# Longer load packets, an earlier start, later weight transfers and a shifted attention schedule in a fused window-attention and softplus-layer kernel

## The chip, the cores and the metric

The kernel runs on one core of a Trainium2 chip. The metric is device time in microseconds (us) of one execution.

The engines are named as the profile names them: PE is TensorE's matmuls, PEld its weight loads, DVE is VectorE, ACT is ScalarE, POOL is GpSimd and SP is SyncE, which mostly issues transfers (SPq is its issuing queue). "Granted clock" (PEclk) is the share of full speed that TensorE was given.

## The reference

Eight batches of attention with 8 heads, 576 positions and head size 64. A position sees a window of 32 to each side; eight "global" positions see everything and are seen by all. The result, as 4608 tokens of 512 features, goes through two matrix products with a softplus between them.

```python
scores = scale * np.matmul(q, k.transpose(0, 1, 3, 2))
mask = np.abs(pos[:, None] - pos[None, :]) <= 32
mask = mask | is_global[:, None] | is_global[None, :]
scores = np.where(mask, scores, -1000000000.0)
... # softmax over keys
x = np.matmul(attn, v)          # -> 4608 tokens x 512
h = x @ w_in                    # 512 -> 2048
g = np.maximum(h, 0.0) + np.log1p(np.exp(-np.abs(h)))
return g @ w_out                # 2048 -> 512
```

## The kernel before

The 4608 tokens are handled as nine tiles of 512 (tile 0 to tile 8). A tile has 16 slots. In slot `s` of tile `n` the kernel emits one sixteenth of the first layer of tile `n` (`mm1`: four 512-column matmuls and two ScalarE passes), one sixteenth of the second layer of tile `n - 1` (`mm2`), and some attention steps of a later batch. Batch 0 must be done before tile 0, batch 1 before tile 1, and so on. Four parts matter here.

All of k, q and v are loaded by position, one head after another, so each contiguous piece is 64 fp32 numbers, 256 bytes:

```python
def load(n, b, eng=None):
    for t in range(NTL):
        s0 = KW * t
        eng.dma_start(out=stage[n][:ST[t], t].rearrange("p (h d) -> p h d", d=D),
                      in_=src[n][b, :, s0:s0 + ST[t], :].rearrange("h s d -> s h d"))
```

There is one staging buffer for each of k, q and v; GpSimd casts it to bf16, and only then can the next batch be loaded into it:

```python
for i, n in enumerate("kqv"):
    at((-22, -20, -17)[i], 1, load, n, b)
    at((-22, -20, -17)[i], 1, load_rows, n, b)
    for t in range(NTL):
        at(-12 + i + t // 3, 0, cast_tile, n, b, t, nc.gpsimd)
for p in range(NP):                      # four pairs of heads
    s = 4 * p - 8
    at(s, 1, transposes, "k", b, p)
    at(s + 1, 0, transposes, "q", b, p)
    at(s + 2, 1, scores, b, p, 0)        # ... exp, mask
    at(s + 4, 1, sums, b, p)             # matmuls with ones
    at(s + 4, 1, values, b, p)           # matmuls with V: these need the cast of v
    ...
    at(s + 5, 1, scale_x, b, p)          # writes xT
at(11, 0, glob_out, b)                   # last writes of xT: tile b waits for them
```

The weights: `w_in` is issued by GpSimd before batch 0's attention, `w_out` just after it, ahead of tile 0:

```python
glob_out(0)
...
for c in range(4):
    nc.gpsimd.dma_start(out=w_out_t[:, 4 * c:4 * c + 4, :], in_=moe_w_out[...])
```

The main loop. In tile 0 there is no second layer, and batch 1 runs at double pace:

```python
for n in range(n_tiles + 1):
    for s in range(16):
        if n < n_tiles: mm1(n, s)
        if n == 0:
            for r in (2 * s - 12, 2 * s - 11):
                attend(1, r, 0); attend(1, r, 1)
            ...                              # and the first steps of batches 2 and 3
            continue
        for b in (n + 1, n + 2, n + 3): attend(b, s - 16 * (b - n - 1), 0)
        mm2(n - 1, s)
        for b in (n + 1, n + 2, n + 3): attend(b, s - 16 * (b - n - 1), 1)
```

The softmax here doesn't subtract the row's maximum and nothing guards it: scores larger than these inputs give would overflow.

Of the kernel before, what the change touches and what calls it, by code (L numbers as in the profile page):

```python
# [11 lines left out]
FP32 = mybir.dt.float32  # L12
# [7 lines left out]
P = 128  # L20
WIN = 32
KW = 120
# [7 lines left out]
SPLIT = 288  # L30

# [6 lines left out]
def kernel(  # L38
# [12 lines left out]
    NP = H // 2  # L51
    d_model, d_ff = moe_w_in.shape
# [16 lines left out]
    ones = const.tile([P, D], BF16)  # L69
    xT = const.tile([P, KD, B * S], BF16)  # L70
# [4 lines left out]
    V1 = [const.tile([P, NTL, d_model], BF16, name=f"V1_{i}") for i in range(2)]  # L75
    stage = {n: const.tile([P, NTL, d_model], FP32, name=f"{n}_f") for n in "kqv"}
    ident_bf = const.tile([P, P], BF16)
    src = {"k": k, "q": q, "v": v}
    grow = {n: nc.dram_tensor(f"{n}_global_rows", (NG, B * H * D), FP32, kind="Internal").ap() for n in "kqv"}


    def load(n, b, eng=None):
        eng = eng or nc.sync
        for t in range(NTL):
            s0 = KW * t
            eng.dma_start(out=stage[n][:ST[t], t].rearrange("p (h d) -> p h d", d=D),  # L86
                          in_=src[n][b, :, s0:s0 + ST[t], :].rearrange("h s d -> s h d"))

    def load_rows(n, b, eng=None):
        eng = eng or nc.sync  # L90
        g = grow[n][:, b * H * D:(b + 1) * H * D]
        eng.dma_start(out=stage[n][KW:P, 0:4], in_=g.unsqueeze(1).to_broadcast([NG, 4, H * D]))
        eng.dma_start(out=stage[n][ST[4]:ST[4] + NG, 4], in_=g)

    def gather(n, eng, regs):
        sv = src[n].rearrange("b h s d -> (b h) s d")
        for g in range(NG):
            eng.dma_start(out=grow[n][g:g + 1].rearrange("o (c d) -> c o d", d=D),
                          in_=sv[:, bass.ds(regs[g], 1), :])
# [3 lines left out]
    def cast_tile(n, b, t, eng):  # L103
        if n == "v":
            kqb[n, b] = V1[b % 2]
        elif t == 0 and b:
            kqb[n, b] = work.tile([P, NTL, d_model], BF16, tag=f"{n}b", bufs=2, name=f"{n}b")
        rows = ST[t] if b == 0 and n != "v" else P
        eng.tensor_copy(kqb[n, b][:rows, t], stage[n][:rows, t])  # L109


    gidx = global_idx.rearrange("(one n) -> one n", one=1).bitcast(I32)
    nc.sync.dma_start(out=idx_r[:], in_=gidx)
    nc.scalar.dma_start(out=idx_i[:], in_=gidx.to_broadcast([P, 2 * NG]))
    nc.scalar.preload_act_table_set("natural_log_exp_and_others")
    for n in "kqv":
        nc.gpsimd.memset(stage[n][96:P, 4], 0.0)
    load("k", 0)
    load("q", 0)

    for n in "kq":
        kqb[n, 0] = work.tile([P, NTL, d_model], BF16, tag=f"{n}b", bufs=2, name=f"{n}b")
        nc.vector.memset(kqb[n, 0][96:P], 0.0)

    ident = work.tile([P, P], FP32, tag="ot", bufs=2, name="ident")
    make_identity(nc, ident[:])
    nc.vector.tensor_copy(ident_bf[:], ident[:])
    nc.vector.memset(ones[:], 1.0)
    low = work.tile([P, NG, NG], FP32, tag="m0")
    nc.gpsimd.memset(low[:], 1.0)  # L130
    nc.gpsimd.affine_select(out=low[:], in_=low[:], compare_op=ALU.is_ge, fill=0.0, base=-1,
                            channel_multiplier=0, pattern=[[1, NG], [-1, NG]])
    kidx_i = work.tile([P, NTL], I32, tag="m3")
    nc.gpsimd.iota(kidx_i[:], pattern=[[KW, NTL]], base=0, channel_multiplier=1)
    vld = const.tile([P, NTL], FP32)
    nc.gpsimd.memset(vld[:], 1.0)
    dgs = []
    for i, (s, c) in enumerate(((KW, slice(0, 4)), (ST[4], slice(4, 5)))):
        nc.gpsimd.affine_select(out=vld[:, c], in_=vld[:, c], compare_op=ALU.is_ge, fill=0.0, base=s - 1,
                                channel_multiplier=-1, pattern=[[0, c.stop - c.start]])  # L140
        dg = work.tile([P, NG], FP32, tag=f"m6{i}")
        nc.gpsimd.memset(dg[:], 1.0)
        nc.gpsimd.affine_select(out=dg[:], in_=dg[:], compare_op=ALU.is_equal, fill=0.0, base=-s,
                                channel_multiplier=1, pattern=[[-1, NG]])
        dgs.append(dg)

    band = work.tile([P, 200], FP32, tag="m7")
    nc.gpsimd.memset(band[:], 1.0)
    nc.gpsimd.memset(band[:, 32:40], 0.0)
# [10 lines left out]
    regs = [  # L160
        nc.values_load(idx_r[0:1, 2 * g:2 * g + 1],
                       engines=[mybir.EngineType.Activation, mybir.EngineType.Pool],
                       min_val=0, max_val=S - 1,
                       skip_runtime_bounds_check_because="positions of the sequence")
        for g in range(NG)
    ]
    gather("v", nc.scalar, regs)
    gather("k", nc.gpsimd, regs)
    gather("q", nc.gpsimd, regs)
    load("v", 0)  # L170
    load_rows("v", 0, nc.scalar)

# [3 lines left out]

# [3 lines left out]
    nc.vector.tensor_tensor(out=same[:], in0=same[:], in1=low[:], op=ALU.mult)  # L180
    uq = work.tile([P, NG], FP32, tag="m2")
    nc.vector.tensor_reduce(out=uq[:], in_=same[:], axis=AX.X, op=ALU.max)
    nc.vector.tensor_scalar(out=uq[:], in0=uq[:], scalar1=-1.0, scalar2=1.0, op0=ALU.mult, op1=ALU.add)

    kidx = work.tile([P, NTL], FP32, tag="m4")
    nc.vector.tensor_copy(kidx[:], kidx_i[:])
    keq = work.tile([P, NTL, NG], FP32, tag="m5")
    nc.vector.tensor_tensor(out=keq[:], in0=kidx[:].unsqueeze(2).to_broadcast([P, NTL, NG]),
                            in1=idx_f[:].unsqueeze(1).to_broadcast([P, NTL, NG]), op=ALU.is_equal)
    onehot = const.tile([P, NTL, NG], BF16)  # L190
    nc.vector.tensor_copy(onehot[:], keq[:])
    akey = const.tile([P, NTL], FP32)
    nc.vector.tensor_reduce(out=akey[:], in_=keq[:], axis=AX.X, op=ALU.max)
    nc.vector.tensor_scalar(out=akey[:], in0=akey[:], scalar1=-1.0, scalar2=1.0, op0=ALU.mult, op1=ALU.add)
    ukey = const.tile([P, 2], FP32)
    for i, dg in enumerate(dgs):
        nc.vector.tensor_tensor(out=dg[:], in0=dg[:], in1=uq[:], op=ALU.mult)
        nc.vector.tensor_reduce(out=ukey[:, i:i + 1], in_=dg[:], axis=AX.X, op=ALU.max)
    nc.vector.tensor_tensor(out=akey[:], in0=akey[:], in1=vld[:], op=ALU.mult)
    masks = [const.tile([P, GW[i]], BF16, name=f"mask{i}") for i in range(2)]  # L200
    for t in range(NTL):
        m = masks[0 if t in GRP[0] else 1]
        c0 = GOFF[t] - (WLO[t] - (128 * t - 40))
        a, vl, u = akey[:, t:t + 1], vld[:, t:t + 1], ukey[:, t // 4:t // 4 + 1]
        if t > 0:
            nc.vector.tensor_scalar(out=m[:, c0:c0 + 40], in0=band[:, 0:40], scalar1=a, scalar2=None, op0=ALU.mult)
        n = ST[t]
        nc.vector.tensor_scalar(out=m[:, c0 + 40:c0 + 40 + n], in0=band[:, 40:40 + n], scalar1=a, scalar2=u,
                                op0=ALU.mult, op1=ALU.add)
        nc.vector.tensor_scalar(out=m[:, c0 + 40 + n:c0 + 48 + n], in0=band[:, 160:168], scalar1=vl, scalar2=None,  # L210
                                op0=ALU.mult)
        if t < 4:
            nc.vector.tensor_scalar(out=m[:, c0 + 168:c0 + 200], in0=band[:, 168:200], scalar1=a, scalar2=None,
                                    op0=ALU.mult)



    def transposes(n, b, p, copy=nc.vector.tensor_copy):
        dst, rows = KT if n == "k" else QT, kqb[n, b]
        ps = psum["pool"].tile([P, 512], FP32, tag="tp", bufs=2 if b == 0 else 1, name="tp")  # L220
        tb = ps[:].bitcast(BF16)
        for t in range(NTL):
            nc.tensor.transpose(out=tb[:, t * P:(t + 1) * P], in_=rows[:, t, p * P:(p + 1) * P], identity=ident_bf[:])  # L223
        if b == 0:
            g = ps[:, 384:384 + NG]
            for t in range(NTL):
                nc.tensor.matmul(out=g, lhsT=rows[:, t, p * P:(p + 1) * P], rhs=onehot[:, t, :],
                                 start=(t == 0), stop=(t == NTL - 1), skip_group_check=True)
        copy(dst[:, p].rearrange("p t c -> p (t c)"), tb[:, 0:NTL * P])  # L229
        if b == 0:  # L230
            copy(dst[:, p, 0:4, KW:P], g.unsqueeze(1).to_broadcast([P, 4, NG]))
            copy(dst[:, p, 4, ST[4]:ST[4] + NG], g)

    exps = {}

    def region(b, name):
        tag, bufs = ({"sc": ("sc", 1), "av": ("av", 2)}[name]) if b == 0 else ("at", 2)
        return psum["pool"].tile([P, 1024], FP32, tag=tag, bufs=bufs, name=name)
# [18 lines left out]

# [63 lines left out]

    gts = {}
# [28 lines left out]
    def attention_slots(b):  # L351
        sl = {}

        def at(s, half, f, *a):
            sl.setdefault((s, half), []).append((f, a))

        for i, n in enumerate("kqv"):
            at((-22, -20, -17)[i], 1, load, n, b)
            at((-22, -20, -17)[i], 1, load_rows, n, b)
            for t in range(NTL):  # L360
                at(-12 + i + t // 3, 0, cast_tile, n, b, t, nc.gpsimd)
        for p in range(NP):
            s = 4 * p - 8
            at(s, 1, transposes, "k", b, p)
# [127 lines left out]
```

## Time and profile before

| | before |
|---|---|
| time, median of 3 runs (range) | 407.64 us (406.65 to 408.45) |
| span of the profiled run | 405.2 us |
| first first-layer matmul (tile 0 can begin) | 44.1 us |
| first second-layer matmul | 103.0 us |
| TensorE busy | 344.7 us |
| packets of all transfers | 124,388 |

The page of the kernel before shows the span in 40 slices of about 10 us. Each digit is a busy share in tenths; for PEclk, the granted clock.

```profile
PE   0367563857999999999999999999999999999985
PEclk9999665798999999999999999999999999999999
DMA  8999999999408771796378558720000101010021
```

For the first 100 us TensorE is only partly busy and the transfers run nearly without a break. After that TensorE is full to the end. So there are three stages: the start, up to the first matmul of tile 0; tile 0; and the rest, where TensorE binds.

The table of windows, cut at the starts of the tiles, puts numbers to this. A tile's start is taken here as its first softplus pass on ScalarE's timeline. The columns are the stretch, its length, the busy time of PE, PEld, DVE, ACT and POOL with instruction counts, the granted clock, the share of the transfer engines (the times of all packets over the time of 16 engines; packets overlap in the records, so it can pass 1), and GB/s. The rows are tile 0, tiles 1 and 2 together, and all that follows.

```profile
core 0: us, PE busy (x) PEld busy (x) DVE busy (x) ACT busy (x) POOL busy (x), PEclk, DMA share, GB/s
46.00:103.90 57.90, 38.32 (x310) 18.41 (x308) 22.04 (x56) 35.49 (x54) 27.70 (x50) 0.78 1.13 189
103.90:179.50 75.60, 73.25 (x605) 37.09 (x604) 34.81 (x92) 61.75 (x97) 17.57 (x42) 1.00 0.58 112
179.50:405.20 225.70, 214.20 (x1468) 103.37 (x1467) 72.56 (x183) 158.55 (x251) 28.89 (x72) 1.00 0.32 74
```

In tile 0 TensorE idles 57.9 − 38.3 = 19.6 us; in tiles 1 and 2 only 2.35 us. What holds tile 0 shows on GpSimd's timeline (start, length, line, operation, count, and in brackets the idle time before it and what ended it):

```profile
42.05 2.04 POOL L319 COPY xT<-xg 128x4 bf16 x8 [15.68 <-DVE xg L314]
44.19 2.97 POOL L436 DMA_DIRECT2D w_out_t<-in_moe_w_out_dram  x4
...
66.33 2.83 POOL L109 CAST V<-v_f 128x512 bf16<-128x512 f32 x5 [12.48 <-DMA v_f<-v_global_rows]
```

The first line finishes batch 0. The second issues all of `w_out`. The third is the cast of batch 1's v, which waited 12.5 us for a transfer and began at 66.3 us.

Last, the page's group of the second layer's matmuls and its queue line. The second layer waited 9.7 us for VectorE's copy of the previous result out of PSUM (`ot`); the packets of queue 1, 118,778 of them with 39.48 MB, took 50.0% of the 16 transfer engines' time over the span.

```profile
q1 hardware_dynamic: 118778, 39.48, 50.0%
...
L343 PE MATMUL o<-w_out_t,gt 128*128 128x512 bf16 x576 | 145.7, 379 | 9.7 <-DVE ot L347 9.7
```

### The profile page before, as it was taken

To read this page: it belongs to the slowest core of one execution; us is meant where nothing else is said; L and a number is where in the kernel's file an instruction comes from. 1 tells how busy PE (TensorE), PEld (TensorE's weight loads), DVE (VectorE), ACT (ScalarE), POOL (GpSimd) and SP (SyncE) were. 2 spreads that over 40 slices of the span, in tenths; PEclk is the share of its full clock that TensorE was granted. 3 is DMA by queue.
4 is the path that set the end of the run, shared out by engine and by line. 5 is a ranking of instruction groups with operands and counts; after the bars stand their busy time and mean duration, and the time that the engine had idled before them with its cause. 6 is when DMAs were issued, how large, how long until landed. Compare 5 with 4: busy or idle time off the path is not lost.

```text
span 405.2 us, 7015 instructions
## 1 busy us (share of the span) xinstructions
PE 344.7 (85%) x2600; PEld 171.5 (42%) x2600; DVE 156.3 (39%) x423; ACT 273.1 (67%) x429; POOL 98.6 (24%) x223
## 2 busy tenths in 40 slices
PE   0367563857999999999999999999999999999985
PEld 0145221433544455455445444444444444444432
DVE  8457120565444444544444444444444201010111
ACT  1068340877988787787878887888788766776600
POOL 5960722364500431234042204220100100000000
PEclk9999665798999999999999999999999999999999
DMA  8999999999408771796378558720000101010021
GB/s 140 206 196 193 185 198 186 177 199 184 82 26 152 152 166 40 153 168 133 77 147 166 93 105 161 160 56 26 28 27 28 53 26 53 28 44 33 28 78 52
DMA packets 124388, 44.60 MB, mean 110 GB/s; under 512 B 114514, under 2 KB 118866, under 8 KB 124354
## 3 DMA queue, kind: packets, MB, share of 16 engines
q1 hardware_dynamic: 118778, 39.48, 50.0%
q0 software_dynamic: 4736, 4.46, 6.6%
q8 instruction: 20, 0.33, 0.3%
q10 hardware_dynamic: 840, 0.22, 0.3%
q14 instruction: 14, 0.11, 0.1%
HBM read 38.90 MB, written 9.83 MB: 120 GB/s over the span
## 4 chain that ended last, share of the span: by engine, by line
PE 63%; ACT 9%; DVE 9%; issue 8%; DMA 5%; SPq 4%; POOL 1%; ACTq 1%; DVEq 0%; POOLq 0%
PE o L343 28%; PE hp L329 22%; ACT ex L250 7%; PE av L273 6%; DVE ot L347 5%; SPq L86 4%; PE tp L223 4%; PE sc L246 3%; DVE ex L255 3%; DMA q_f<-q_global_rows 2%; DMA q_f<-in_q_dram 1%; DMA v_global_rows<-in_v_dram 1%; DMA v_f<-v_global_rows 1%; ACT QT L383 1%; POOL V L109 1%
## 5 line engine op out<-in xcount | busy, mean ns | idle before, releaser
L329 PE MATMUL hp<-xT,w_in_t 128*128 128x512 bf16 x576 | 154.1, 393 | 3.8 <-POOL xT L319 3.8
L343 PE MATMUL o<-w_out_t,gt 128*128 128x512 bf16 x576 | 145.7, 379 | 9.7 <-DVE ot L347 9.7
L332 ACT ACTIVATE e<-hp 128x512 f32<-128x512 f32 x144 | 86.1, 598 | 63.7 <-PE hp L329 61.3
L333 ACT ACTIVATE gt<-e 128x512 bf16<-128x512 f32 x144 | 90.7, 630 | 4.6
L343 PEld LDWEIGHTS <-gt 128*128 128x128 bf16 x576 | 55.2, 97 | 77.6 <-issue 18.8
L329 PEld LDWEIGHTS <-w_in_t 128*128 128x128 bf16 x576 | 53.5, 100 | 69.1 <-issue 15.1
L255 DVE TENSOR_TENSOR ex<-ex,mask 128x1008 bf16<-128x1008 bf16 x64 | 43.7, 684 | 54.2 <-ACT ex L250 53.2
L250 ACT ACTIVATE ex<-sc 128x1008 bf16<-128x1008 f32 x64 | 56.1, 920 | 4.7 <-PE sc L246 4.6
L347 DVE COPY ot<-o 128x512 f32<-128x512 f32 x36 | 24.7, 686 | 72.5 <-PE o L343 72.5
L319 POOL COPY xT<-xg 128x4 bf16 x64 | 12.9, 202 | 141.2 <-DVE xg L314 137.8
L291 ACT ACTIVATE rz<-av 128x616 f32<-128x616 f32 x32 | 21.8, 683 | 19.2 <-DVE KT L229 14.6
L109 POOL CAST V<-v_f 128x512 bf16<-128x512 f32 x40 | 23.8, 644 | 42.1 <-DMA v_f<-v_global_rows 36.0
L246 PE MATMUL sc<-QT,KT 64*128 64x200 bf16 (+2 forms) x320 | 21.3, 258 | 9.9 <-DVE xT L306 2.8
L304 DVE TENSOR_TENSOR xT<-av,rz 128x480 bf16<-128x480 f32 x32 | 21.0, 656 | 22.0 <-ACT rz L295 21.9
L229 DVE COPY KT<-tp 128x640 bf16<-128x640 bf16 x32 | 15.6, 486 | 32.8 <-PE tp L223 32.8
L109 POOL CAST qb<-q_f 128x512 bf16<-128x512 f32 x35 | 20.9, 642 | 29.9 <-DMA q_f<-q_global_rows 25.5
L223 PE MATMUL tp<-ident_bf,kb 128*128 128x128 bf16 x160 | 16.8, 233 | 12.2 <-DVE kb L109 10.4
L273 PE MATMUL av<-ex,V 128*64 128x200 bf16 (+4 forms) x384 | 19.7, 236 | 8.4 <-POOL V L109 7.8
L273 PE MATMUL av<-ex,ones 128*64 128x200 bf16 (+4 forms) x384 | 20.4, 239 | 4.8 <-DVE ex L255 4.7
L282 DVE TENSOR_REDUCE gs<-av 128x8 f32<-128x32 f32 x64 | 11.9, 185 | 31.8 <-ACT rz L291 31.5
L223 PE MATMUL tp<-ident_bf,qb 128*128 128x128 bf16 x160 | 17.2, 234 | 7.5 <-DVE qb L109 5.0
L295 ACT ACTIVATE rz<-rz 128x616 f32<-128x616 f32 x32 | 22.5, 704 | 0.2
(69 smaller groups left out, 167.4 us busy)
## 6 DMA issues: line engine op xcount, KB each, us to landing
out_dram<-ot SPq DMA_DIRECT2D x36, 256.0 KB
k_f<-in_k_dram SPq DMA_DIRECT2D x32, 240.0 KB
q_f<-in_q_dram SPq DMA_DIRECT2D x32, 240.0 KB
v_f<-in_v_dram SPq DMA_DIRECT2D x32, 240.0 KB
w_in_t<-in_moe_w_in_dram POOLq DMA_DIRECT2D x4, 512.0 KB, 12.2
w_out_t<-in_moe_w_out_dram POOLq DMA_DIRECT2D x4, 512.0 KB, 12.2
k_f<-in_k_dram SPq DMA_DIRECT2D x8, 192.0 KB
q_f<-in_q_dram SPq DMA_DIRECT2D x8, 192.0 KB
```

What stands on the lines that cost most here:

```text
L109: eng.tensor_copy(kqb[n, b][:rows, t], stage[n][:rows, t])
L223: nc.tensor.transpose(out=tb[:, t * P:(t + 1) * P], in_=rows[:, t, p * P:(p + 1) * P], identity=ident_bf[:])
L246: nc.tensor.matmul(out=sc[:, e, GOFF[t]:GOFF[t] + w], lhsT=KT[r, p, t, :], rhs=QT[r, p].rearrange("p t c -> p (t c)")[:, WLO[t]:WHI[t]], s ...
L250: nc.scalar.activation(out=ex[:], in_=sc[:, :, 0:GW[grp]], func=ACTF.Exp, scale=SCALE)
L255: nc.vector.tensor_tensor(out=ex[:], in0=ex[:], in1=masks[grp][:].unsqueeze(1).to_broadcast([P, 2, GW[grp]]), op=ALU.mult)
L273: nc.tensor.matmul(out=av[64 * e:64 * e + 64, OFF + lo:OFF + hi], lhsT=weights(t, e), rhs=exps[p, grp][:, e, c:c + hi - lo], start=(lo in ...
L295: nc.scalar.activation(out=RZ[p][:], in_=RZ[p][:], func=ACTF.Exp, scale=-1.0)
L329: nc.tensor.matmul(out=hp[:], lhsT=w_in_t[:, kd, kf * P:(kf + 1) * P], rhs=xT[:, kd, n * NT:(n + 1) * NT], start=(kd == 0), stop=(kd == KD ...
L332: nc.scalar.activation(out=e[:], in_=hp[:], func=ACTF.Exp)
L333: nc.scalar.activation(out=gts[n][:, kf, :], in_=e[:], func=ACTF.Ln, bias=1.0)
L343: nc.tensor.matmul(out=op[:], lhsT=gts[n][:, kf, i * P:(i + 1) * P], rhs=w_out_t[:, kf, :], start=(kf == 0), stop=(kf == KF - 1))
L347: nc.vector.tensor_copy(ot[:], op[:])
```

## The change

The intent, in five points.

1. k and q are loaded as runs of six tokens, 1536 contiguous bytes, instead of 256. v stays as it was. Since a partition now holds six positions, the transposes become six of 96 columns, and the copies out of PSUM are strided; the global columns of later batches come from one table that is built in slot 12 of tile 0.
2. Batch 0 is loaded, cast and computed one pair of heads at a time, so that its scores can begin after the first pair.
3. `w_in` is issued inside batch 0's attention, and `w_out` in slots 1 and 3 of tile 0.
4. From batch 4 on each attention step is one slot later, so that VectorE's mask does not stand ahead of the output copy. Batches 2 and 3 are squeezed to double pace.
5. Ten junk matmuls run before batch 0's first transposes and ten before tile 0, to warm the clock.

The core of the diff, with cuts marked:

```diff
+    def load_runs(n, b, heads=slice(0, H)):
+        nc.sync.dma_start(out=runs[n][:, heads], in_=src[n][b, heads].rearrange("h (p r) d -> p h (r d)", r=RUN))
...
-        for t in range(NTL):
-            nc.tensor.transpose(out=tb[:, t * P:(t + 1) * P], in_=rows[:, t, p * P:(p + 1) * P], identity=ident_bf[:])
+        for r in range(RUN):
+            nc.tensor.transpose(out=tb[:, r * NQ:(r + 1) * NQ], in_=rows[:, r, p * P:(p + 1) * P],
+                                identity=ident_bf[:NQ, :NQ])
...
+    LOAD = {2: (2, 3, 5), 3: (20, 20, 20), 4: (30, 30, 31)}
+    CAST = {1: 1, 2: 16, 3: 26}
+    START = {1: 6, 2: 20, 3: 30}
...
-            s = 4 * p - 8
+            r = 4 * p - 7
...
+                if b in START:
+                    at(START[b] + (r + 7) // 2, (r + 7) % 2, f, *a)
+                else:
+                    at(g0 + r, half, f, *a)
...
+    warm(10)
     transposes("k", 0, 0)
...  # batch 0, pair by pair; load_w_in(p) inside; batch 1's k and q issued at p == 1
     glob_out(0)
+    load_v(1)
+    load_v_rows(1)
+    for n in "kq":
+        gather(n, nc.sync)
+    load_global_columns()
+    warm(10)
...
-    for c in range(4):
-        nc.gpsimd.dma_start(out=w_out_t[...], in_=moe_w_out[...])
...
     for n in range(n_tiles + 1):
         for s in range(16):
             if n < n_tiles:
                 mm1(n, s)
+            if n == 0 and s in (1, 3):
+                load_w_out(s - 1)
+                load_w_out(s)
+            if n == 0 and s == 12:
+                for m in "kq":
+                    global_columns(m)
+            attend(16 * n + s, 0)
+            if n:
+                mm2(n - 1, s)
+            attend(16 * n + s, 1)
```

## The prediction

> **What bounds the kernel now.** Three stages, read from the timeline. (1) Batch 0's attention: 0 to 44.15 us, when the first first-layer matmul starts. (2) Tile 0 with batch 1's attention: to about 102 us (first second-layer matmul at 103.0). (3) Tiles 1 to 8 and the last second layer: to 405.2 us. In stage 3 TensorE binds: the table of windows has it busy 38.6 to 38.8 of every 40 us; by the chain of waits four slots take 9.42 us with attention, 6.98 without. In stages 1 and 2 it is busy about 55 of 100 us, the DMA engines are saturated (share 1.0 to 1.25), and the timeline shows GpSimd's casts of q, v and the next k waiting 1.0, 12.5 and 4.5 us for transfers. The granted clock is 0.57 to 0.74 from 40 to 80 us: four 512-column matmuls take 1.7 to 1.9 us instead of 0.86.
>
> **What the change does.**
> - k and q of a batch come as 1536 packets of 1536 B instead of 9216 of 256 B. Packet records show 24 ns for 256 B, 100 ns for 2 KB; I estimate 70 ns for 1536 B, so k, q and v of a batch cost about 14 us of all 16 engines, not 21. This agrees with the Trainium skill, "DMA: Bandwidth & Descriptors", Specifications (line rate needs at least 512 B).
> - Batch 0 starts with one head pair: 0.59 MB instead of 2.36. Scores began at 20.1 us; now 10 to 11. Then the v rows (gathered to memory, read back on a queue that waits) and GpSimd's casts of pairs 2 and 3 hold it: values of pair 0 near 22 instead of 29.6. With about 4.6 us a pair as before: first first-layer matmul at 34 to 40 us, 37 in the middle.
> - Twenty warm-up matmuls fill idle time and lift the clock; the skill's "TensorE: Matmul & The Clock Gate", Part 1, says idle is the throttled state. The trace agrees: granted 0.5 in four stretches between 51 and 106 us.
> - Tile 0: ScalarE needs 16 x 1.23 us for softplus plus 4 x 3.1 for attention, 32 us; w_in, batch 1 and w_out compete (about 41 us of all engines), so batch 1's v is somewhat late. 37 us instead of 58.
> - Stage 3: attention one slot later puts masks after the output eviction; TensorE waited 6.3 us for that copy between 110 and 300 us. Gain about 5 us, minus six 96-column transposes for five of 128, strided PSUM copies (estimate 0.95 us against 0.49), batches 2 and 3 squeezed into ten slots each. Net 2 us: 301.
>
> Sum 37 + 37 + 301 = 375: **374 us, 362 to 388**. Faster by over 2%: 0.96; within 2%: 0.03; slower: 0.01.
>
> **What would show it.** First first-layer matmul near 37 us, first second-layer matmul near 74, then about 301 to the end. About 63 thousand DMA packets. Granted clock near 1.0 from 40 us on. TensorE's idle time before the eviction nearly gone except in the last tile.
>
> **What would make it wrong.** GpSimd does more in the start (masks, casts); a VectorE mask took 2.14 us instead of 0.57 beside GpSimd's v cast at 23.2. If that repeats, batch 0 ends at 42 or later. Late w_in or v stalls tile 0 and drops the clock. Squeezed batches may stall TensorE 1 us a pair. Well-fed loads could end tile 0 at 66 us.

## The result

The changed kernel takes 402.57 us (median of 4 runs, 401.58 to 402.77), the kernel before 407.14 us in the same rounds (405.77 to 408.45). The ratio is 0.9883, with a 95% interval of 0.9845 to 0.9922: within 2%. Ratios here are the mean time of one kernel's fast runs over the mean of the other's of the same rounds, so not quite the ratio of the medians quoted. The measured time lies outside the predicted range of 362 to 388 us.

The same slices of the page of the kernel after:

```profile
PE   7299726587989889999999999999999999999985
PEclk9999965978999999999999999999999999999999
DMA  7979991890792980567157546720001001010021
```

The same table of windows of the kernel after, again cut at tile 0, tiles 1 and 2, and the rest:

```profile
37.70:94.90 57.20, 34.85 (x305) 17.33 (x304) 19.62 (x66) 30.48 (x49) 14.35 (x25) 0.77 0.84 154
94.90:181.30 86.40, 79.69 (x696) 40.24 (x695) 48.30 (x125) 66.95 (x103) 39.95 (x88) 0.99 0.62 135
181.30:400.00 218.70, 210.85 (x1494) 102.45 (x1492) 87.34 (x212) 158.47 (x251) 38.30 (x97) 1.00 0.29 74
```

The balance, from the tile starts of both timelines (the last two rows part the third window at the start of tile 7, at 328.5 us before and 323.7 us after):

| stretch | before, us | after, us | difference |
|---|---|---|---|
| start, to tile 0 | 46.0 | 37.7 | −8.3 |
| tile 0 | 57.9 | 57.2 | −0.7 |
| tiles 1 and 2 | 75.6 | 86.4 | +10.8 |
| tiles 3 to 6 | 149.0 | 142.4 | −6.6 |
| tile 7 to the end | 76.7 | 76.3 | −0.4 |
| span | 405.2 | 400.0 | −5.2 |

The start and the late tiles did gain. Tile 0 did not shrink, although its attention work got lighter (batch 2 used to begin in it), and tiles 1 and 2 grew. In tiles 1 and 2 TensorE is busy 6.4 us longer (79.69 − 73.25) and idle 4.4 us longer (86.40 − 79.69 = 6.71, against 2.35).

GpSimd's timeline of the kernel after answers to the one shown before:

```profile
34.54 2.03 POOL L350 COPY xT<-xg 128x4 bf16 x8 [7.46 <-DVE xg L345]
36.66 1.49 POOL L470 DMA_DIRECT2D w_out_t<-in_moe_w_out_dram  x2
...
43.83 1.48 POOL L470 DMA_DIRECT2D w_out_t<-in_moe_w_out_dram  x2
...
62.00 2.84 POOL L119 CAST V<-v_f 128x512 bf16<-128x512 f32 x5 [14.67 <-DMA v_f<-v_global_rows]
```

Batch 0 is done 7.5 us earlier, but the cast of batch 1's v begins only 4.3 us earlier, at 62.0 us. And `w_out`, which was to come later, is issued from 36.66 us, where it used to be issued at 44.19: it moved later in slots and earlier in time, because tile 0 itself moved. TensorE's timeline shows what that costs: the sums of pair 0 run at 52 us, and then the values wait for V.

```profile
52.01 0.91 PE L304 MATMUL av<-ex,ones 128*64 128x160 bf16 x12
62.66 0.35 PE L304 MATMUL av<-ex,V 128*64 128x160 bf16 x2 [9.74 <-POOL V L119]
...
65.81 1.87 PE L378 MATMUL hp<-xT,w_in_t 128*128 128x512 bf16 x4
```

The four matmuls in the last line take 1.87 us; with a full clock four take 1.04 us on this timeline. The wait has also kept the clock low: when it is filled with junk matmuls (below), the same four take 1.02 us. But it is not the only cause. The clock had been low once before the wait, when four took 1.89 us at 49.71 us.

SP's timeline shows v's transfers in the queue. The first line is the five transfers of batch 1's v, the third and the last the same five transfers for later batches:

```profile
25.28 31.14 SPq L94 DMA_DIRECT2D v_f<-in_v_dram  x5
56.47 1.36 SPq L98 DMA_DIRECT2D v_f<-v_global_rows  x1
...
140.29 4.43 SPq L94 DMA_DIRECT2D v_f<-in_v_dram  x5
...
180.47 4.13 SPq L94 DMA_DIRECT2D v_f<-in_v_dram  x5
```

The same five instructions take 4.1 to 4.4 us to issue late in the kernel, and 31.1 us around the start of tile 0, when the share of the transfer engines is above 1 (1.19 from 50 to 60 us). Batch 2's five, left out here, took 15.2 us from 73.07 us. Finally, the queue line and the group of the second layer:

```profile
q1 hardware_dynamic: 57518, 39.00, 42.4%
...
L392 PE MATMUL o<-w_out_t,gt 128*128 128x512 bf16 x576 | 146.8, 381 | 3.1 <-DVE ot L396 3.1
```

Half the packets are gone, but the queue's share of engine time fell only from 50.0% to 42.4%. The wait for the output copy fell from 9.7 to 3.1 us, as intended.

### The profile page after: what moved, and what is told of

Same layout as the page of the kernel before. It is cut to its first block, busy times and chain, and to the rows that moved or that the text cites. A ratio compares the mean times of both kernels' runs of the same rounds, so it can differ in the third digit from the quotient of the medians.

```text
span 400.0 us, 7285 instructions
## 1 busy us (share of the span) xinstructions
PE 350.8 (88%) x2748; PEld 176.8 (44%) x2748; DVE 177.0 (44%) x485; ACT 273.8 (68%) x434; POOL 114.2 (29%) x263
## 2 busy tenths in 40 slices
DMA packets 62048, 43.72 MB, mean 109 GB/s; under 512 B 40510, under 2 KB 56958, under 8 KB 62014
## 3 DMA queue, kind: packets, MB, share of 16 engines
q1 hardware_dynamic: 57518, 39.00, 42.4%
## 4 chain that ended last, share of the span: by engine, by line
PE 61%; issue 14%; DMA 12%; POOL 5%; DVE 3%; SPq 2%; ACT 2%; POOLq 0%; ACTq 0%
PE o L392 28%; PE hp L378 24%; DMA v_f<-in_v_dram 6%; PE av L304 4%; DMA q_f<-in_q_dram 3%; PE tp L246 2%; DMA v_f<-v_global_rows 2%; PE sc L278 2%; POOL V L119 2%; POOL qb L116 1%; DVE ot L396 1%; ACT ex L282 1%; POOL xT L350 1%; SPq L90 1%; SPq L94 1%
## 5 line engine op out<-in xcount | busy, mean ns | idle before, releaser
L378 PE MATMUL hp<-xT,w_in_t 128*128 128x512 bf16 x576 | 152.1, 388 | 4.9 <-POOL xT L350 4.4
L287 DVE TENSOR_TENSOR ex<-ex,mask 128x1008 bf16<-128x1008 bf16 x64 | 46.2, 729 | 32.3 <-ACT ex L282 31.2
L119 POOL CAST V<-v_f 128x512 bf16<-128x512 f32 (+1 forms) x45 | 26.3, 626 | 44.9 <-DMA v_f<-v_global_rows 41.7
L257 DVE COPY KT<-tp 128x480 bf16<-128x480 bf16 x32 | 20.9, 654 | 33.0 <-PE tp L246 17.5
L322 ACT ACTIVATE rz<-av 128x616 f32<-128x616 f32 x32 | 21.8, 680 | 15.4 <-PE av L304 14.9
L304 PE MATMUL av<-ex,V 128*64 128x200 bf16 (+4 forms) x384 | 21.4, 248 | 10.5 <-POOL V L119 10.5
L257 DVE COPY QT<-tp 128x480 bf16<-128x480 bf16 x28 | 18.4, 658 | 25.2 <-PE tp L251 14.8
L116 POOL CAST kb<-k_f 96x1024 bf16<-96x1024 f32 (+1 forms) x23 | 24.3, 1088 | 10.5 <-DMA k_f<-in_k_dram 10.5
L116 POOL CAST qb<-q_f 96x1024 bf16<-96x1024 f32 (+1 forms) x23 | 24.0, 1068 | 8.9 <-DMA q_f<-in_q_dram 8.9
L304 PE MATMUL av<-ex,ones 128*64 128x200 bf16 (+4 forms) x384 | 22.1, 248 | 4.3 <-DVE ex L287 3.4
```

The lines of the kernel that those rows point to most:

```text
L116: eng.tensor_copy(o, i)
L119: eng.tensor_copy(V1[b % 2][:, t, cols], v_f[:, t, cols])
L257: copy(dst[:, p, 0:4, 0:KW].rearrange("p t (q r) -> p t q r", r=RUN), spread[:, 0:4 * NQT].rearrange("p (t q) r -> p t q r", q=NQT))
L287: nc.vector.tensor_tensor(out=ex[:], in0=ex[:], in1=masks[grp][:].unsqueeze(1).to_broadcast([P, 2, GW[grp]]), op=ALU.mult)
L304: nc.tensor.matmul(out=av[64 * e:64 * e + 64, OFF + lo:OFF + hi], lhsT=weights(t, e), rhs=exps[p, grp][:, e, c:c + hi - lo], start=(lo in ...
L378: nc.tensor.matmul(out=hp[:], lhsT=w_in_t[:, kd, kf * P:(kf + 1) * P], rhs=xT[:, kd, n * NT:(n + 1) * NT], start=(kd == 0), stop=(kd == KD ...
```

## The experiments

Four reasons were possible for tile 0 not shrinking. **A**: batch 1's v comes late because `w_out` takes the transfer engines ahead of it. **B**: the fallen clock costs the time, whatever made it fall. **C**: the work itself, ScalarE's or TensorE's, needs the time. **D**: the long packets are not as cheap as was thought. Separately, the one-slot shift and the early start were to be weighed. "After" below means the changed kernel; each edit is one to it unless another base is named.

### w_out behind the cast of v (theory A)

```diff
-            if n == 0 and s in (1, 3):
-                load_w_out(s - 1)
-                load_w_out(s)
...
             attend(16 * n + s, 1)
+            if n == 0 and s in (6, 7):      # behind the V casts in GpSimd's order
+                load_w_out(2 * s - 12)
+                load_w_out(2 * s - 11)
```

> Only the four w_out transfers move: from slots 1 and 3 of tile 0 to slots 6 and 7, behind the v casts of batch 1 on GpSimd. Theory A (tile 0 is held by the arrival of batch 1's v, and v is late because 4.2 MB of w_out share the DMA engines with it): the v cast of batch 1 starts near 50 us instead of 62.0, the second tile's first matmul comes near 82 to 84 instead of 93.0, and the whole time falls by 8 to 11 us, to about 393. Theory B (the serial work after v, not v, sets the end of tile 0): the cast comes earlier, but the second tile starts within 3 us of 93. Theory C (w_out is not what v competes with; k, q and w_in are): the cast starts after 58 us.

Measured: 394.52 us, ratio to the kernel before 0.9715 (0.9673 to 0.9757). From GpSimd's timeline:

```profile
51.02 2.83 POOL L119 CAST V<-v_f 128x512 bf16<-128x512 f32 x5 [5.41 <-DMA v_f<-v_global_rows]
53.79 2.96 POOL L470 DMA_DIRECT2D w_out_t<-in_moe_w_out_dram  x4
```

The cast of v began at 51.0 instead of 62.0 us. That fits the packet records: the 4160 packets of 1024 bytes, of which 4096 are the weights' and half of these `w_out`'s, took 97.8 ns each on average, so `w_out` is an estimated 2048 × 97.8 ns / 16 = 12.5 us of all 16 engines. Tile 0 shrank from 57.2 to 49.7 us, and the whole by 8 us. A is confirmed. Whether `w_in` and batch 1's k and q hold v up as well was not tested. Tile 0 is still far from 37 us.

### No load of batch 1's v at all (the whole of A)

```diff
     glob_out(0)
-    load_v(1)
-    load_v_rows(1)
```

> Wrong on purpose: batch 1's v is not loaded, its cast reads batch 0's. That takes the wait for v away whole. Theory A: TensorE's idle 9.7 us before the values of pair 0 vanishes, tile 0 takes 44 to 46 us instead of 56.4, the profile spans about 389. Theory B: tile 0 still takes over 52 us.

Measured: 390.23 us (one run, state unknown). This kernel uses batch 0's v for batch 1 and is wrong on purpose; it nevertheless passed the comparison with the reference, whose tolerance does not see it, so for kernels of this case "correct" says little about v. The rows are tile 0 and tiles 1 and 2:

```profile
37.90:80.20 42.30, 28.66 (x305) 15.30 (x304) 19.52 (x66) 30.48 (x49) 13.44 (x24) 0.96 0.98 178
80.20:169.30 89.10, 81.23 (x696) 40.75 (x695) 49.85 (x125) 67.17 (x103) 41.42 (x90) 0.98 0.63 131
```

Tile 0 takes 42.3 us, 14.9 less than in after, with the same softplus work and attention. So the work itself (C) does not need 57 us. The window row splits the 14.9 us into 6.2 us of busy time (the same 305 matmuls are busy 28.66 us instead of 34.85) and 8.7 us of idle time, but this is not a split by cause, since slow matmuls also fill what would be other waits (in tile 0 TensorE waits 2.9 us for VectorE's mask here, 1.8 us in after). The timeline shows where the time is lost. The first-layer matmuls that follow the values of pair 0, which start at 65.81 us in after, start here at

```profile
53.33 1.02 PE L378 MATMUL hp<-xT,w_in_t 128*128 128x512 bf16 x4
```

So some 12.5 of the 14.9 us are lost by the time pair 0 has its values: the wait for v, and the casts of V, which come one at a time. The other 2 us or so are added later, where after's matmuls run in part at a lower clock. (Without v's load SP also issues everything behind it earlier; in slot 12 of tile 0, where that could matter, TensorE waits 1.3 and 0.7 us for the global rows in both kernels.) But tiles 1 and 2 take 89.1 us instead of 86.4, so 2.7 us are given back there. 1.2 of these are tile 1's matmuls, busy 40.67 us instead of 39.47 at a granted clock of 0.96 instead of 0.99; another 1.2 are idle time in tile 2.

### Junk matmuls while v is awaited (theory B)

```diff
             step(r + 4, 1, sums, b, p)
+            if b == 1 and p == 0:
+                step(r + 4, 1, fill, 40)
             step(r + 4, 1, values, b, p)
```

> Forty junk matmuls are put where TensorE waits for v of batch 1 in tile 0, so its clock should not fall. If the low clock (0.56 from 60 to 70 us, 0.71 from 80 to 90) costs time on the chain after v, tile 0 ends 2 to 4 us earlier and the time falls by as much. If the chain after v is latency of ScalarE, VectorE and hand-overs, it changes by less than 1 us.

Measured: 402.12 us, ratio 0.9897 (0.9849 to 0.9945): the same as after. The clock did rise; the stretch from 60 to 70 us, granted 0.56 in after, shows 1.00, and tile 0 shrank by 2.6 us to 54.6. Tiles 1 and 2 took 1.7 of it back, 88.1 us instead of 86.4, and the rest went at the start and in the tiles after them:

```profile
60.00:70.00 10.00, 7.90 (x71) 3.80 (x70) 3.12 (x10) 3.34 (x5) 2.84 (x5) 1.00 0.17 31
...
92.50:180.60 88.10, 80.79 (x696) 40.52 (x695) 49.31 (x125) 66.91 (x102) 40.23 (x87) 0.98 0.61 132
```

The four matmuls behind the values of pair 0 answer to those of 1.87 us:

```profile
65.57 1.02 PE L378 MATMUL hp<-xT,w_in_t 128*128 128x512 bf16 x4
```

B by itself is refuted: a warm clock in the wait, without the data, shortens tile 0 by 2.6 us and gains nothing in the end. The clock was still low at other places (granted 0.59 and 0.56 from 78 to 82 us, 0.50 from 92 to 94 us), so this run does not say what a full clock throughout would be worth.

### Attention without the one-slot shift from batch 4 on

```diff
-                    at(g0 + r, half, f, *a)
+                    at(g0 + r - 1, half, f, *a)
```

> Attention of batches 4 to 7 goes back one slot, as before the change; batches 1 to 3 keep their places. If the shift is what took tiles 3 to 5 from 38.3 to 36.6 us, these tiles return to about 38.3, TensorE's idle before the second layer (waiting for the output eviction) goes from 3.1 to 8 us or more, and the time rises by 5 to 6 us, to about 408. If the gain in tiles 3 to 5 has another source (transposes, GpSimd copies), they stay below 37.2.

Measured: 411.69 us, ratio 1.0121 (1.0078 to 1.0164). Tiles 3, 4 and 5 take 39.4 us each instead of 36.6, and the group of the second layer has its wait back:

```profile
L392 PE MATMUL o<-w_out_t,gt 128*128 128x512 bf16 x576 | 147.0, 381 | 9.9 <-DVE ot L396 9.9
```

The shift is worth (1.0121 − 0.9883) × 407 = 9.7 us. The mechanism was as expected, the size not: 5 to 6 us had been expected. From tile 3 to tile 6 the change as a whole gained only 6.6 us, so by subtraction the rest of the new attention costs some 3 us there. VectorE's longer strided copies are a likely reason, but no run took that apart.

### Small packets everywhere (theory D)

```diff
-        nc.sync.dma_start(out=runs[n][:, heads], in_=src[n][b, heads].rearrange("h (p r) d -> p h (r d)", r=RUN))
+        o = runs[n][:, heads].rearrange("p h (r d) -> p h r d", r=RUN)
+        i = src[n][b, heads].rearrange("h (p r) d -> p h r d", r=RUN)
+        for r in range(RUN):
+            nc.sync.dma_start(out=o[:, :, r], in_=i[:, :, r])
```

> k and q are loaded into the same places, but in six transfers each, one token of the run at a time, so in packets of 256 B again; nothing else moves. The packet records say that 1536 B cost 105 ns and 256 B 24 ns, so k and q of a batch take 13.8 us of all 16 engines instead of 10.1, 3.7 us a batch. If the DMA engines bound the start of tile 0, batch 0 and batch 1 together put the v cast of batch 1 about 7 us later than 62.0 and the time rises by 5 to 8 us, to about 409. If the packet size hardly matters (bytes from memory bind), the v cast stays within 2 us of 62 and the time within 2 us of 402.6.

Measured: 422.43 us, ratio 1.0396 (1.0329 to 1.0464). The experiment missed its aim. SP's timeline, this kernel first and then after:

```profile
1.35 2.81 SPq L93 DMA_DIRECT2D k_f<-in_k_dram  x6
```

```profile
1.33 0.35 SPq L90 DMA_DIRECT2D k_f<-in_k_dram  x1
```

Each load became six transfers, which take 2.81 us to issue instead of 0.35, and batch 0 has eight such loads. The first first-layer matmul came at 52.9 us, 16 us later. Eight times 2.5 us is more than the whole loss, so issue time alone can explain it (argued from these numbers, not tested), and the size of the packets had to be tested apart from batch 0.

### Small packets from batch 1 on (theory D, apart from the start)

The same edit, but only for `b > 0`; batch 0 keeps the single transfer.

> As e5, but batch 0 keeps its long packets, so the start is as after the change: only k and q of batches 1 to 7 come in packets of 256 B. The issue on the queue is not short of time there (v's issue already waits until 56 us for room). If packets are what the DMA engines spend their time on, v's cast moves from 62.0 to about 65 to 67, and the time rises by 3 to 5 us, to about 406.5. If bytes from memory bind, less than 1.5 us.

Measured: 407.66 us (404.19 to 409.9), ratio 0.9999 (0.9947 to 1.0051). The cast of v began 4 us later than in after, at 66.0 us, as expected:

```profile
66.03 2.85 POOL L125 CAST V<-v_f 128x512 bf16<-128x512 f32 x5 [11.30 <-DMA v_f<-v_global_rows]
```

Tile 0 took 62.5 us, and the whole is 4.7 us slower than after ((0.9999 − 0.9883) × 407). The six transfers still cost more to issue than one, so this is the worth of the long runs as they are used, issue time included: about as much as the whole net gain of the change.

The packet records say why it is not more: 1536-byte packets took 105.5 ns on average, not the 70 ns estimated. k, q and v of a batch cost (1536 × 105.5 + 4608 × 23.8) / 16 ns = 17.0 us of all engines instead of 13,824 × 24.0 / 16 = 20.7 us; 14 us had been predicted. So D holds in part: the long packets do save time, but 3.7 us a batch instead of 7.

### A late start (is the early start worth anything?)

```diff
-    warm(10)           # before tile 0
+    warm(45)
```

> Thirty-five more junk matmuls stand before tile 0, so that its first matmul comes about 7.5 us later, at 44, where it came before the change; the transfers do not wait for TensorE. Theory A (batch 1's v sets when tile 0 ends, so the earlier start is swallowed): the v cast stays at 62, the second tile starts within 2 us of 93, the time rises by less than 2 us. Theory B (tile 0 has a length of its own): all comes 6 to 8 us later, about 409.

Measured: 402.59 us, ratio 0.9923 (0.9879 to 0.9967). Tile 0's first matmul came at 43.0 instead of 36.6 us, the cast of v where it was, and tile 1 began at 94.2 us, where after had 94.9. (The releaser in brackets is the profile's inference; it names the transfer that SP issues next behind v's rows.)

```profile
62.05 2.84 POOL L119 CAST V<-v_f 128x512 bf16<-128x512 f32 x5 [14.72 <-DMA k_global_rows<-in_k_dram]
```

The span is 400.0 us in both. The medians agree (402.59 and 402.57); the ratios differ by 1.6 us, but their intervals overlap. From the cast of v to tile 1 it took 32.2 us instead of 32.9. In the kernel after, then, 6.4 us of early start are worth nothing that can be told from the noise: they pass in the wait for v. (The junk matmuls may hide a little: the clock of tile 0 was 0.83 instead of 0.77.)

### The global columns later as well (based on the kernel with w_out behind v)

With v early, TensorE waited 3.6 us for `q_rows_bf` and 1.6 us for `k_rows_bf` in slot 12 of tile 0, where the table of global columns is built. First needed by batch 2, it can be built in tile 1.

```diff
-            if n == 0 and s == 12:
+            if n == 1 and s == 1:
                 for m in "kq":
                     global_columns(m)
```

> On top of e1 (w_out late): the transposes of the global columns of k and q move from slot 12 of tile 0 to slot 17, in tile 1. In e1 slot 12 took 10.3 us, with 5.2 us of idle TensorE before those transposes. If they stand on the chain of tile 0, the second tile comes 4 to 6 us earlier than e1's 84.8 and the time falls from 394.5 to about 390. If another wait of the same chain takes their place, less than 2 us.

Measured: 389.73 us, ratio 0.9587 (0.9544 to 0.9629), about 5 us less than its base. Tile 0 takes 41.5 us, as little as without any load of v. Tiles 1 and 2 take 89.4:

```profile
38.00:79.50 41.50, 30.10 (x293) 15.36 (x296) 18.19 (x62) 30.43 (x48) 14.02 (x25) 0.88 0.98 183
79.50:168.90 89.40, 80.17 (x692) 40.66 (x703) 50.30 (x129) 66.92 (x102) 39.98 (x89) 0.98 0.67 144
```

In the stretch of tiles 1 and 2, the waits of TensorE for VectorE's `xT` ahead of the scores, where two steps of a squeezed batch stand close, are six of 0.7 us:

```profile
PE sc L278 <- DVE xT L337: 4.2, 6, 0.7
```

### Batches 2 and 3 spread out (based on the kernel just shown)

```diff
-    START = {1: 6, 2: 20, 3: 30}
+    START = {1: 6, 2: 18, 3: 30}
+    PACE = {1: 0.5, 2: 0.667, 3: 0.75}
...
-                    at(START[b] + (r + 7) // 2, (r + 7) % 2, f, *a)
+                    h = int(2 * START[b] + PACE[b] * (2 * (r + 7) + half))
+                    at(h // 2, h % 2, f, *a)
```

> On top of e7: batch 2 starts at slot 18 and takes 13 slots instead of 20 and 10, batch 3 takes 14 slots from 30 instead of 10. Tiles 1 and 2 took 43.7 and 43.0 us after the change, 38.0 and 38.4 before, with TensorE idle 6 us between 110 and 180. If the squeezing makes those waits, they shrink: tiles 1 and 2 together 3 to 6 us shorter than in e7, the time about 386. If they are just the work that tile 0 no longer does, the two tiles change by less than 1.5 us.

Measured: 383.72 us (382.21 to 386.85), ratio 0.9470 (0.9413 to 0.9526). The window rows and the wait that answer to the last ones:

```profile
38.00:78.80 40.80, 28.98 (x293) 15.04 (x297) 18.19 (x62) 30.48 (x49) 13.30 (x24) 0.92 0.97 184
78.80:161.50 82.70, 77.19 (x692) 40.04 (x703) 50.59 (x129) 66.78 (x103) 41.37 (x88) 1.00 0.71 157
```

```profile
PE sc L278 <- DVE xT L337: 1.2, 3, 0.5
```

In these two traces tiles 1 and 2 lost 6.7 us: 3.7 us of idle time (89.4 − 80.17 = 9.2 became 82.7 − 77.19 = 5.5) and 3.0 us of busy time for the same 692 matmuls, with the clock at 1.00 instead of 0.98. Not all of this is the edit's. The profiled run was the fastest of four, and by the ratios the gain is 4.8 us. Tile 2 went from 43.5 to 39.0 us and takes 39.0 us in the two later runs with this schedule too, so these 4.5 us stand: the squeezed batches were a cost of their own. Tile 1 went from 45.9 to 43.7 us, but took 45.2 and 44.6 us in those two (a late start, and batch 1 one slot earlier), where the clock was low at its start; in the profiled run it was not. Against the kernel before, tiles 1 and 2 are still 7.1 us longer, of which 3.9 us is busy time (77.19 − 73.25).

**This version beats both kernels.**

### A late start on the best version

On the kernel just shown, the junk matmuls before tile 0 went from 10 to 45.

> The same thirty-five junk matmuls as in e8, now on top of e9, where batch 1's v no longer keeps TensorE waiting (0.8 us). After the change itself the later start cost nothing (e8). Theory A says that the early start pays once v is early: e10 is 5 to 7 us slower than e9, about 389.5. If something else that is fixed in time (the last loads of batch 1's q, or w_out) sets tile 0's end in e9 too, it is less than 2 us slower.

Measured: 387.19 us (384.64 to 387.99), ratio 0.9503 (0.9460 to 0.9546). The medians differ by 3.5 us, the ratios by 1.3 us, and the intervals overlap. 5 to 7 us had been expected. Tile 0 then takes 37.6 instead of 40.8 us, so part of the delay is absorbed. Whether the rest is real is not settled: the best version's own four runs spread from 382.2 to 386.9 us, with mean clocks between 0.989 and 0.951.

### Batch 2 earlier (on the best version)

Batch 2 was moved into tile 0 from slot 12 on (`START` 12, `CAST` 9), with the global rows gathered after its loads and the table built later.

> On top of e9: batch 2's k and q are loaded before the global rows are gathered, its global columns come from the one-hot product, and its attention runs from slot 12 of tile 0, as part of it did before the change; batch 3 from slot 27. TensorE is idle about 10 of the 40 us of e9's tile 0, and work of batch 2 could fill it: tiles 1 and 2 fall to 38 or less, the time to about 379. If batch 2's v or w_out come too late for that, tile 0 grows by as much as tiles 1 and 2 lose, and the time stays within 2 us of 383.7, or rises.

Measured: 395.89 us, ratio 0.9740 (0.9705 to 0.9774), 11 us slower than its base. Tile 0 grew to 54.4 us, and tiles 1 and 2 did not shrink (84.3 us instead of 82.7). Batch 2's v was cast only at 84.1 us, but the trace does not show theory A again. TensorE waited 3.1 us for V in tiles 0 to 2, in seven waits of at most 1.4 us:

```profile
PE av L304 <- POOL V L119: 3.1, 7, 1.4
```

Of the 13.6 us by which tile 0 grew, 8.3 are busy time (370 matmuls, 37.24 us, at a clock of 0.86, instead of 293, 28.98 us, at 0.92) and 5.3 are idle time in many waits of at most 1.7 us, most of them for VectorE. Why the moved work did not fit into the idle time of tile 0, and why tiles 1 and 2 got no shorter without it, is open.

### Batch 1 one slot earlier (on the best version)

`START[1]` from 6 to 5, in five rounds.

> On top of e9: batch 1's attention starts at slot 5 instead of 6, so that a whole slot of first-layer work is left after its last step. In e9 TensorE waits 3.6 us at the start of tile 1 for the last global columns of batch 1's output. If that tail is exposed only because nothing is left to do, tile 1 comes 1 to 3 us earlier and the time is 381 to 383; if slot 5 only waits longer for batch 1's q and v (whose transfers end when they did), the gain is under 1 us.

Measured: 384.1 us (382.14 to 384.52, 6 runs), ratio 0.9410 (0.9372 to 0.9449). The median is that of the best version; by the ratios it is 2.4 us faster, but the intervals overlap. TensorE's wait at the start of tile 1 went from 3.60 to 2.73 us, yet in the profiled run tile 0 takes 41.7 us, with a clock of 0.85 instead of 0.92. A gain is neither shown nor excluded.

## Why the prediction was wrong

**The start: right.** The first first-layer matmul was predicted at 37 us and came at 36.6; scores were predicted at 10 to 11 us and began at 9.0; the values of pair 0 were predicted near 22 us and began at 22.07. The cause named was right too: TensorE's longest wait there, 5.3 us, was for GpSimd's cast of k.

**Tile 0: the step that failed.** The prediction said: "w_in, batch 1 and w_out compete (about 41 us of all engines), so batch 1's v is somewhat late. 37 us instead of 58." From its first matmul at 36.62 us to the first second-layer matmul at 94.64 us tile 0 took 58.0 us, 21.0 more than predicted. The lateness of v was named, but the 37 us are ScalarE's 32 us and some 5 us for all else. ScalarE's work was right (30.48 us busy), but it did not set the tile's length: TensorE stood 9.74 us for V, and ScalarE with it. A sum could have shown the size. `w_in`'s first transfer was issued at 22.44 us, and from there the prediction's own 41 us of all engines end at about 63 us (an estimate, made afterwards); v was cast at 62.00. Taking `w_out` from in front of v moved v by 11.0 us; taking v's load away brought tile 0 to 42.3 us. So about 15 of the 21 us go with v's load: 12.5 us until pair 0 has its values, and about 2 us of slow matmuls after it. Nor did the edit that was to move `w_out` out of the way do so: it was issued at 36.66 us instead of 44.19, since the slots had themselves moved.

The remaining 4 to 5 us of tile 0 (41 to 42 us with v out of the way against 37) are open. ScalarE is busy 30.5 us of the best version's 40.8, so it does not fill the tile. TensorE is idle 11.8 us of it; the longest waits are 3.6 us at the end for the last columns of batch 1's output, 2.7 us in seven waits for VectorE's mask, and 1.5 us for V.

**The rest: 301 us predicted, 305.4 measured.** The shift removed the wait for the output copy, as predicted, and was worth more than thought (9.7 us). The squeeze of batches 2 and 3, which the prediction named as "may stall TensorE 1 us a pair", happened: six waits of 0.7 us, and spreading them out gained 4.8 us by the ratios. Tiles 1 and 2 also hold more attention than before, since batch 2 no longer begins in tile 0; that the 6.4 us of extra busy time is this work is read from the two schedules and the counts (696 matmuls against 605), not shown by a run.

**The packets: the count right, the cost not.** About 63 thousand were predicted and 62,048 counted. A 1536-byte packet cost 105.5 ns instead of the estimated 70.

**The clock: wrong.** "Near 1.0 from 40 us on" was predicted; in the five 10 us stretches from 50 to 100 us it was 0.67, 0.56, 0.95, 0.71 and 0.83. The wait for v is one reason (filling it raised the clock from 0.56 to 1.00 between 60 and 70 us and gained nothing in the end), but not the only one. In stretches of 2 us the trace grants 0.57 and 0.58 from 48 to 52 us, before that wait, and 0.50 to 0.55 from 80 to 86 us, after the waits of slot 12. The first ten junk matmuls did not warm it as predicted: six transposes behind them took 0.66 us, at 25.81 us still, against 0.42 later. (The prediction's "between 51 and 106 us" counts from the trace's own zero; from the start of the span the four stretches lie between 41 and 96 us.)

The sum was 375 against a span of 400.0 us: −0.4 at the start, +21.0 in tile 0, +4.4 after it.

**Left open.** Why part of what tile 0 gains is given back in tiles 1 and 2 (1.7 of 2.6 us with the junk matmuls, 2.7 of 14.9 us without v's load); a lower clock at the start of tile 1 is part of it. What the early start is worth once v is on time. What sets tile 0's 41 us in the best version. What the junk matmuls and the pair-by-pair start of batch 0 are worth each: no run took them out alone.

## What to carry to other kernels

An earlier start is worth nothing if the next stage waits for a transfer that cannot come earlier: list the bytes in the order in which the queues will serve them and ask which one the next stage waits for, and put that wait into the sum. When a schedule is in slots, "later" in the code can be earlier in time, so keep bulk weights behind the small load that work is waiting for, tied to that load's consumer and not to a slot. Look at the wait before its symptom: here a clock kept warm while the data was missing gained nothing. And when a trace differs from another in the clock, compare the ratios of all runs too before putting its whole gain down to the edit.

## What the Trainium skill lacked or had wrong

- "DMA: Bandwidth & Descriptors", Specifications, gives 512 B as the least transfer for line rate and about 27 GiB/s per engine. Here 256-byte packets took 23.8 ns (10.7 B/ns), 1536-byte packets 105.5 ns (14.6 B/ns) and 2048-byte ones 95.7 ns (21.4 B/ns). Packets six times as long, and well above 512 B, brought only about 36% more bytes per ns in this mix of traffic. Neither this section nor the page's account of small descriptors has the time of such packets in mixed traffic, which is what the estimate of 70 ns needed.
- The same page, "Issuing engines are not separate DMA queues", says that transfers of different issuing engines run on the same 16 engines and interleave. This case agrees and adds a size: GpSimd's `w_out` put off SP's v by 11.0 us (62.0 against 51.0 us).
- "Perfetto Trace Analysis", What "DMA-bound" means, reads an issuing sequencer that is solid with transfer slices as descriptor generation, not data movement. Here the same five issues of v took 31.1 us behind a backlog and 4.1 to 4.4 us later. So the length of the slice went with the traffic around it. What helped was taking other bytes out of v's way: with `w_out` behind it the five took 21.6 us, and v's cast came 11.0 us earlier. Larger descriptors for v were not tried.
- "TensorE: Matmul & The Clock Gate", Part 1, gives about 3.4 us of sustained work, on a free-running window, to release the throttle. The ten junk matmuls at the very start lasted 4.45 us (445 ns each, against 343 ns each for the ten before tile 0), and the six transposes behind them still took 0.66 us against 0.42 later: they did not lift the clock in time. (With a window that runs freely this is no contradiction.) In the same stretch the granted-clock row shows 9 in every slice, so its first slices are not to be relied on here; this agrees with that page's warning that such records cannot be trusted alone.
